# Float64 weights to float32: a bit shift of the upper word plus the scaled lower word, in place, with one work array per job

## The chip, the cores and the metric

The kernel runs on one core of a Trainium2 chip. Its time is the device time of one execution in microseconds (us); of several runs the median counts. The engines are TensorE (PE, matrix products, with its weight loads as PEld), VectorE (DVE), ScalarE (ACT), GpSimd (POOL) and SyncE (SP), which issues most of the transfers.

## The reference

The input x has 8 batches of 3008 x 256 float32. A Fourier transform runs over both axes, its real part goes through a feed-forward layer with a piecewise activation. The weights come as float64 and are used as float32 values:

```
X = np.fft.fft(x, axis=1)
X = np.fft.fft(X, axis=2)
x = X.real.astype(np.float32).reshape(24064, 256)
h = x @ w_in                       # 256 x 2048
g = np.where(h >= 1, h, np.where(h <= -1, 0.0, (h + 1) ** 2 / 4))
return (g @ w_out).astype(np.float32)   # 2048 x 256
```

## The kernel before

The transform over the sequence is split into two stages of small products (3008 = 64 x 47), the one over the 256 columns is folded into `w_in`. The feed-forward layer is cut into **units**: one batch, one of three chunks of tokens, 128 of the 2048 inner columns. There are 384 units. For each of them TensorE computes two products u and v of the first layer (`gemm1`, line 552, three passes each, in three PSUM banks by the name `uv` that are used in turn), VectorE computes `us` from the first (line 555), then the two signs `h` = us - uv and us + uv (lines 558, 559), ScalarE two passes over h (`a`), VectorE the activation step `g` out of a and h (line 574, later 579, which writes into h), and TensorE adds the second layer's product into four banks `acc` (`gemm2`, line 635) some units later. From unit 20 on, `g` is split into a rounded part `gh` (ScalarE) and a rest `gl` (GpSimd, line 598). While a batch is in the units, the transform of the next one is done in pieces in between.

Batch 0 has nothing to hide behind, so at the start the transform of batch 0, the conversion of the weights and the first units are woven together by hand. `START` is a list of steps ahead of unit 0, `AHEAD`, `AMID` and `STEPS` give the steps inside the units 0 to 32. A step is a letter and a number; up to unit 24 the order in which steps are written out is the order of issue on every engine (`pin`). The letters that matter here are: `l` load a piece of weights, `x` load a piece of x, `y` and `g` fold such a piece (VectorE and GpSimd), `p` a piece of the transform on TensorE (p0 to p7 first stage, p8 the extra row, p9 on the second stage), `w` and `z` copies of its result, `q` splits the second stage's result into `pqh` and `pql`, `F` and `f` the products that fold a converted half of `w_in` with the column transform (line 342) and round it to `wh` on ScalarE, `s` its lower part `wl` on VectorE, `u`, `O`, `Q` the rounded and the lower part of `w_out`.

The weights are 16 **jobs** of 128 x 512 float64 values each, read as pairs of 32-bit words, lower word first (`raw`). Jobs 0, 1, 4, 5, 8, 9, 12, 13 are of `w_in`, the others of `w_out`. Before, a job runs as follows. `a`: VectorE takes the 20 upper mantissa bits and the 11 exponent bits out of the upper word into the two halves of a work array `cv` (lines 253, 258). `b`: ScalarE turns the mantissa into 1.xxx and the exponent into the bits of a power of two, with clamping at both ends, in three passes (lines 267 to 269). `c`: VectorE adds the lower word times 2^-52 to the mantissa and the sign to the power (lines 274, 275). `d` on GpSimd or `v` on VectorE (jobs 0, 1, 2): mantissa times power (line 289). The work arrays lie in buffers lent by the names `h`, `a` and `gl`.

Of the kernel before, what the change touches and what calls it, by code (L numbers as in the profile page):

```python
# [22 lines left out]
P = 128  # L23
# [5 lines left out]
CH = 512  # L29
# [12 lines left out]
def _constants():  # L42
# [30 lines left out]


START = (
# [3 lines left out]
)  # L79
AHEAD = {1: "v2 G0"}  # L80
AMID = {0: "p11", 1: "p12 D1 E1 q11 q12", 3: "p13 q13", 6: "p14 q14", 7: "f2", 11: "f4", 16: "f6"}
STEPS = {
    0: "c2",
    1: "b3",
    2: "c3 d3",
    3: "a4 b4",
    4: "a5 c4 d4 b5",
    5: "c5 d5",
    7: "f3 a8 s2 b8",
    8: "s3 r1 a9 c8 d8 b9",  # L90
    9: "a6 c9 d9 b6",
    10: "c6 d6",
    11: "f5 a12 s4 b12",
    12: "s5 r2 a13 c12 d12 b13",
    13: "a7 c13 d13 b7",
    14: "c7 d7 u0",
    15: "a10 b10 L0 L1 u1 Q0",
    16: "s6 u2 Q1 |",
    17: "f7 a11 c10 d10 b11",
    18: "s7 r3 c11 d11 L2",  # L100
    19: "a14 Y0 b14 L3 u3 O2",
    20: "a15 c14 d14 b15",
    21: "O3 c15 d15 u4",
    22: "O4 Y1 u6 u5",
    23: "O6 O5 u7",
    24: "O7",
# [20 lines left out]
def fft_ffn_kernel(ctx: ExitStack, tc: tile.TileContext, x, xn, cst, w_in, w_out, out):  # L127
    nc = tc.nc

    wts = ctx.enter_context(tc.tile_pool(name="wts", bufs=1))  # L130
    sb = ctx.enter_context(tc.tile_pool(name="sb", bufs=1))
# [128 lines left out]
    def convert_fields(n):  # L260
        convert_mantissa(n)
        convert_exponent(n)

    def convert_floats(n):
        man, exp = (cv[n][0][:, i] for i in range(2))
        expf = exp.bitcast(F32)
# [10 lines left out]
    def convert_scale(n, eng):  # L277
        t, _ = cv.pop(n)
        kind, q, *_ = jobs[n]
        man, exp = (t[:, i].bitcast(F32) for i in range(2))  # L280
        dst = man
        if kind == "in":
            f32s[n] = man
        else:
            if q % 2 == 0:
                pair = sb.tile([P, 2, CH], F32, tag="gl", name=f"wo_{q // 2}", bufs=4)
                wo32[q], wo32[q + 1] = pair[:, 0], pair[:, 1]
            dst = wo32[q]
# [81 lines left out]
    s1, s2, zn = {}, {}, {}  # L370
# [302 lines left out]
    n1 = XC  # L673

    def piece_sums(n):
# [31 lines left out]
        "G": activate,
# [32 lines left out]
    for i in range(n_units + LAG):  # L740
        if i < n_units:
            b, r = divmod(i, per)
# [18 lines left out]
        first, _, then = STEPS.get(i, "").rpartition("|")  # L761
# [109 lines left out]
```

## Time and profile before

| | us |
|---|---|
| median of 3 runs | 1712.65 |
| lowest and highest run | 1712.25, 1715.63 |
| profiled execution | 1712.49 |
| its span, from the first to the last instruction | 1710.7 |
| busy in the span: PE, PEld, DVE, ACT, POOL | 1705.1, 1389.1, 1353.6, 1335.6, 1123.2 |

The 1.8 us between span and time lie around the instructions. An engine's busy time is the union of its instructions; on PE an instruction that waits in the pipeline counts as busy, so its busy time is no measure of its load. The TensorE clock was granted in full (2.4 GHz) over the whole span.

### The profile page before, as it was taken

The page shows a single profiled execution, that of the slowest core. Times are in us where ns is not written, and L with a number is a line of the kernel's source. Part 1 is how long each engine was busy: PE and PEld are TensorE (multiplying, and loading weights), DVE is VectorE, ACT ScalarE, POOL GpSimd, SP SyncE. Part 2 cuts the span into 40 slices and gives each one's busy share as a digit, 9 for nine tenths or more (in the row PEclk, how much of TensorE's full clock was granted, in tenths as well). Part 3 has the DMA queues.
Part 4 walks back from the last instruction along what each step waited for, and adds up shares of the span by engine and source line. Part 5 has one row for each costly group of instructions (what it writes and reads, how often), then busy time and mean ns, then how long its engine had stood idle before and what let it go on. Part 6 is the DMA issues. An engine that isn't in the chain of part 4 may idle for free.

```text
span 1710.7 us, 21453 instructions
## 1 busy us (share of the span) xinstructions
PE 1705.1 (100%) x7736; PEld 1389.1 (81%) x7736; DVE 1353.6 (79%) x1762; ACT 1335.6 (78%) x1541; POOL 1123.2 (66%) x921
## 2 busy tenths in 40 slices
PE   9999999999999999999999999999999999999999
PEld 6557888888888888888888888888888888888887
DVE  8998788877777787777777778777777777778776
ACT  6878777877788777887787877887778877777775
POOL 1125678856887568865688657886577855566664
PEclk9999999999999999999999999999999999999999
DMA  8123111100011000110010100101001010000000
GB/s 322 48 98 109 59 57 56 61 13 31 25 45 60 20 25 25 56 48 20 25 62 20 59 8 25 62 24 56 19 13 62 1 36 31 1 25 24 1 25 25
DMA packets 35466, 76.29 MB, mean 45 GB/s; under 512 B 4640, under 2 KB 13344, under 8 KB 35360
## 3 DMA queue, kind: packets, MB, share of 16 engines
q1 hardware_dynamic: 35180, 74.79, 12.6%
q8 instruction: 61, 1.00, 0.2%
q14 instruction: 45, 0.37, 0.1%
q10 hardware_dynamic: 180, 0.14, 0.0%
HBM read 47.10 MB, written 27.81 MB: 44 GB/s over the span
## 4 chain that ended last, share of the span: by engine, by line
PE 99%; DMA 0%; DVE 0%; SPq 0%; ACT 0%; issue 0%
PE acc L635 62%; PE uv L552 31%; PE s L509 3%; PE s L391 2%; PE s L396 1%; PE wps L342 1%; DMA raw<-in_moe_w_in_dram 0%; PE delta L321 0%; PE ny L482 0%; DVE cv L289 0%; DVE o L653 0%; DVE cv L275 0%; DVE y L153 0%; DVE cv L274 0%; DVE o L641 0%; DVE cv L253 0%
## 5 line engine op out<-in xcount | busy, mean ns | idle before, releaser
L598 POOL TENSOR_TENSOR gl<-h,gh 128x512 fp32r<-128x512 f32 (+1 forms) x724 | 908.9, 1276 | 449.2 <-PE acc L635 220.2
L564 ACT ACTIVATE a<-h,biases 128x1024 f32<-128x1024 f32 (+1 forms) x385 | 436.0, 1133 | 265.6 <-DVE h L559 264.1
L635 PE MATMUL acc<-gh,woh 128*128 128x512 f32 (+1 forms) x1456 | 574.3, 394 | 0.0
L635 PE MATMUL acc<-gl,woh 128*128 128x512 f32 (+1 forms) x1456 | 570.0, 391 | 0.0
L635 PE MATMUL acc<-gh,wol 128*128 128x512 f32 (+1 forms) x1456 | 566.9, 389 | 0.0
L555 DVE SCALAR_TENSOR_TENSOR us<-nyb,delta,uv 128x512 f32<-128x512 f32 (+1 forms) x384 | 282.9, 737 | 287.9 <-PE uv L552 287.3
L579 DVE SCALAR_TENSOR_TENSOR h<-a,h 128x1024 f32<-128x1024 f32 (+1 forms) x365 | 477.2, 1308 | 2.6 <-ACT a L565 2.1
L582 ACT ACTIVATE gh<-h 128x1024 fp32r<-128x1024 f32 (+1 forms) x365 | 379.8, 1040 | 46.6 <-DVE h L579 29.5
L565 ACT ACTIVATE a<-a 128x1024 f32<-128x1024 f32 (+1 forms) x385 | 395.1, 1026 | 1.1
L635 PEld LDWEIGHTS acc<-gl,woh 128*128 128x128 f32 x1456 | 274.3, 188 | 57.1
L635 PEld LDWEIGHTS acc<-gh,wol 128*128 128x128 f32 x1456 | 273.7, 188 | 56.4
L635 PEld LDWEIGHTS acc<-gh,woh 128*128 128x128 f32 x1456 | 273.8, 188 | 53.5
L552 PE MATMUL uv<-pqh,wh 128*128 128x512 f32 (+1 forms) x768 | 306.3, 399 | 0.0
L558 DVE TENSOR_TENSOR h<-us,uv 128x512 f32<-128x512 f32 (+1 forms) x384 | 260.3, 678 | 52.0 <-DVE us L555 1.5
L552 PE MATMUL uv<-pql,wh 128*128 128x512 f32 (+1 forms) x768 | 299.3, 390 | 0.0
L552 PE MATMUL uv<-pqh,wl 128*128 128x512 f32 (+1 forms) x768 | 298.9, 389 | 0.0
L559 DVE TENSOR_TENSOR h<-us,uv 128x512 f32<-128x512 f32 (+1 forms) x384 | 257.5, 671 | 0.0
L552 PEld LDWEIGHTS uv<-pqh,wl 128*128 128x128 f32 x768 | 144.2, 188 | 35.0 <-issue 4.6
L552 PEld LDWEIGHTS uv<-pqh,wh 128*128 128x128 f32 x768 | 144.2, 188 | 33.4 <-issue 3.6
L552 PEld LDWEIGHTS uv<-pql,wh 128*128 128x128 f32 x768 | 144.1, 188 | 30.2 <-DVE pql L220 0.4
L166 POOL TENSOR_TENSOR x<-x 120x256 f32<-120x256 f32 x72 | 68.2, 948 | 4.6 <-DVE h L579 3.5
L635 PE MATMUL acc<-g,wo 128*128 128x482 f32 (+1 forms) x160 | 69.6, 577 | 0.0
(80 smaller groups left out, 783.5 us busy)
## 6 DMA issues: line engine op xcount, KB each, us to landing
x<-in_xn_dram SPq DMA_DIRECT2D x36, 512.0 KB, 3.5
out_dram<-o SPq DMA_DIRECT2D x26, 512.0 KB, 2.8
x<-in_x_dram SPq DMA_DIRECT2D x16, 512.0 KB, 6.1
out_dram<-o SPq DMA_DIRECT2D x14, 482.0 KB, 2.9
nyb<-nyr SPq DMA_DIRECT2D x24, 256.0 KB, 3.2
raw<-in_moe_w_in_dram SPq DMA_DIRECT2D x4, 512.0 KB
raw<-in_moe_w_out_dram SPq DMA_DIRECT2D x4, 512.0 KB, 10.5
part<-o SPq DMA_DIRECT2D x4, 512.0 KB, 3.0
```

The costliest lines, as they stand in the source:

```text
L166: return nc.gpsimd.tensor_tensor(t[:, r], t[:, r], t[:, r + 1], op=ALU.add).ins
L509: nc.tensor.matmul(pt[:, i], z[:, c], rm, start=True, stop=True)
L552: nc.tensor.matmul(t[:, :n], w[m][:, cols], r[:, m, :n], start=(j == 0), stop=(j == 2))
L555: nc.vector.scalar_tensor_tensor(us, nyb[b, k][:, :n], delta[:, f : f + 1], uv[0], op0=ALU.mult, op1=ALU.add)
L558: nc.vector.tensor_tensor(h[:, 0], us, uv[1], op=ALU.subtract)
L559: last_h = nc.vector.tensor_tensor(h[:, 1], us, uv[1], op=ALU.add).ins
L564: nc.scalar.activation(a[:, sg], h[:, sg], AF.Relu, bias=half, scale=0.5)
L565: nc.scalar.activation(a[:, sg], a[:, sg], AF.Square)
L579: g = nc.vector.scalar_tensor_tensor(h[:, sg], a[:, sg], 1.0, h[:, sg], op0=ALU.min, op1=ALU.max).ins
L582: nc.scalar.activation(gh[:, sg], h[:, sg], AF.Copy)
L598: ins = nc.gpsimd.tensor_tensor(gl[:, sg], h[:, sg], gh[:, sg].bitcast(F32), op=ALU.subtract).ins
L635: nc.tensor.matmul(acc[:, :n], w, g[:, sg], start=(begin and j == 0), stop=(last and j == len(terms) - 1))
```

## The change

A float64 whose exponent lies in the range of float32 becomes a float32 when its upper word is shifted left by three bits and sign and top exponent bit are put back; what is then missing are the mantissa bits of the lower word, worth (lower word) x 2^-52 x (power of two of the value). The changed kernel computes this with one work array of 128 x 512 per job, and otherwise in place in `raw`. `e` is ScalarE's `Abs` of the upper word read as a float, `T` ScalarE's scaling of the lower word (`b` is both). `a` is now two chained steps on VectorE, a clamp of the float and shift-and-mask of its bits. `J` joins sign and bits, `K` takes sign and exponent of the joined word, that is the signed power of two (`c` is both). `M` multiplies the lower word with the power (VectorE for jobs 0 and 1, GpSimd for the others), and a sum gives the value (`v` on VectorE for jobs 0, 1, 2; `d` is scale and sum on GpSimd). The two halves of a `w_in` block and two neighbouring jobs of `w_out` share a buffer by the name `gl` (`h` for jobs 0 and 1).

```
-WORK = {1: "a", 3: "a", 4: "gl", 5: "gl", 7: "a", 8: "gl", 9: "gl", 11: "a", 12: "gl", 13: "gl", 15: "a"}
-BUFS = {"h": 4, "a": 3, "gl": 4}
+BUFS = {"h": 4, "gl": 4}
+SMALLEST, LARGEST = (float(np.uint32(n).view(np.float32)) for n in (0x38000000, 0x47EFFFFF))
...
-    def convert_mantissa(n):
-        raw = raws.pop(n)
-        tag = WORK.get(n, "h")
-        t = sb.tile([P, 2, CH], U32, tag=tag, name=f"cv_{n}", bufs=BUFS[tag])
-        high = raw[:, :, 1]
-        nc.vector.tensor_scalar(t[:, 0], high, 0xFFFFF, None, op0=ALU.bitwise_and)
-        nc.vector.tensor_scalar(t[:, 1], high, 20, 0x7FF, op0=ALU.logical_shift_right, op1=ALU.bitwise_and)
...
+    def convert_size(n):
+        raw = raws.pop(n)
+        t = work_tile(n)
+        cv[n] = t, raw
+        nc.scalar.activation(t.bitcast(F32), raw[:, :, 1].bitcast(F32), AF.Abs)
+    def convert_tail(n):
+        low = cv[n][1][:, :, 0]
+        nc.scalar.activation(low.bitcast(F32), low, AF.Copy, scale=2.0**-52)
...
     def convert_floats(n):
-        nc.scalar.activation(man.bitcast(F32), man, AF.Copy, scale=2.0**-20, bias=1.0)
-        nc.scalar.activation(expf, exp, AF.Relu, bias=above, scale=-1.0)
-        nc.scalar.activation(exp, expf, AF.Relu, bias=top, scale=-(2.0**23))
+        convert_size(n)
+        convert_tail(n)
+    def convert_fields(n):
+        nc.vector.tensor_scalar(size, size, SMALLEST, LARGEST, op0=ALU.max, op1=ALU.min)
+        nc.vector.tensor_scalar(t, t, 3, 0x3FFFFFF8, op0=ALU.logical_shift_left, op1=ALU.bitwise_and)
+    def convert_head(n):
+        nc.vector.scalar_tensor_tensor(high, high, 0xC0000000, t, op0=ALU.bitwise_and, op1=ALU.bitwise_or)
+    def convert_power(n):
+        nc.vector.tensor_scalar(t, raw[:, :, 1], 0xFF800000, None, op0=ALU.bitwise_and)
     def convert_join(n):
-        nc.vector.scalar_tensor_tensor(man, raw[:, :, 0], 2.0**-52, man, op0=ALU.mult, op1=ALU.add)
-        nc.vector.scalar_tensor_tensor(exp, raw[:, :, 1], 0x80000000, exp, op0=ALU.bitwise_and, op1=ALU.bitwise_or)
+        convert_head(n)
+        convert_power(n)
+    def convert_scale(n):
+        if n < 2:
+            nc.vector.scalar_tensor_tensor(low, raw[:, :, 0], 2.0**-52, t.bitcast(F32), op0=ALU.mult, op1=ALU.mult)
+        else:
+            nc.gpsimd.tensor_tensor(low, low, t.bitcast(F32), op=ALU.mult)
-        eng.tensor_tensor(dst, man, exp, op=ALU.mult)
+    def convert_sum(n, eng):
+        eng.tensor_tensor(t, high, low, op=ALU.add)
+    def convert_rest(n):
+        convert_scale(n)
+        convert_sum(n, nc.gpsimd)
...
-    8: "s3 r1 a9 c8 d8 b9",
+    8: "s3 r1 a8 c8 d8 b9",
```

The tables move steps of the jobs. Three places show what that does to the order of issue. The first is VectorE at the start, from the end of job 0 to the third fold of x: `x_1` and `x_2` (of 96 x 512) are the folds y1 and y2, `y_0` the fold y0. Before:

```order
L289 TENSOR_TENSOR cv_115<-cv_115 128x512
L153 TENSOR_TENSOR y_0_130<-x_0_95 96x512
L158 TENSOR_TENSOR x_0_95<-x_0_95 96x64
L274 SCALAR_TENSOR_TENSOR cv_121<-raw_92,cv_121 128x512
L275 SCALAR_TENSOR_TENSOR cv_121<-raw_92,cv_121 128x512
L153 TENSOR_TENSOR x_1_98<-x_1_98 96x512
L289 TENSOR_TENSOR cv_121<-cv_121 128x512
L153 TENSOR_TENSOR x_2_100<-x_2_100 96x512
```

The same place of VectorE's order now:

```order
L311 TENSOR_TENSOR f_in_112<-raw_87 128x512
L152 TENSOR_TENSOR y_0_121<-x_0_92 96x512
L157 TENSOR_TENSOR x_0_92<-x_0_92 96x64
L278 TENSOR_SCALAR f_in_112<-f_in_112 128x512
L279 TENSOR_SCALAR f_in_112<-f_in_112 128x512
L285 SCALAR_TENSOR_TENSOR raw_89<-raw_89,f_in_112 128x512
L290 TENSOR_SCALAR f_in_112<-raw_89 128x512
L152 TENSOR_TENSOR x_1_95<-x_1_95 96x512
L301 SCALAR_TENSOR_TENSOR raw_89<-raw_89,f_in_112 128x512
L311 TENSOR_TENSOR f_in_112<-raw_89 128x512
L152 TENSOR_TENSOR x_2_97<-x_2_97 96x512
```

Ahead of the fold of `x_1` two joins of job 1 became four chained steps, and between the folds of `x_1` and `x_2` one step became two; before, the fields of job 1 stood further up, ahead of the joins of job 0.

The second place is VectorE in unit 8, from its activation step `g` to the `us` of unit 9. Before:

```order
L574 SCALAR_TENSOR_TENSOR g_568<-a_532,h_529 128x1024
L363 SCALAR_TENSOR_TENSOR wl_71<-wps_541,biases,wh_69 128x512
L253 TENSOR_SCALAR cv_581<-raw_wol 128x512
L258 TENSOR_SCALAR cv_581<-raw_wol 128x512
L274 SCALAR_TENSOR_TENSOR cv_545<-raw_wol,cv_545 128x512
L275 SCALAR_TENSOR_TENSOR cv_545<-raw_wol,cv_545 128x512
L555 SCALAR_TENSOR_TENSOR us_598<-nyb_2_187,delta,uv_0_590 128x512
```

And now:

```order
L604 SCALAR_TENSOR_TENSOR g_556<-a_523,h_520 128x1024
L393 SCALAR_TENSOR_TENSOR wl_71<-wps_532,biases,wh_69 128x512
L278 TENSOR_SCALAR f_in_537<-f_in_537 128x512
L279 TENSOR_SCALAR f_in_537<-f_in_537 128x512
L285 SCALAR_TENSOR_TENSOR raw_wol<-raw_wol,f_in_537 128x512
L290 TENSOR_SCALAR f_in_537<-raw_wol 128x512
L585 SCALAR_TENSOR_TENSOR us_585<-nyb_2_181,delta,uv_0_577 128x512
```

The count is the same; before, the first pair was of job 9 and the second of job 8, now all four are of job 8 and each works on what the one ahead left. Jobs 4, 5, 6, 7, 9, 12, 13 stand in units 4 to 14 in the same way.

The third place is GpSimd from the last fold of x at the start to the jobs of the first units. Before, with one pass for a job:

```order
L153 TENSOR_TENSOR x_6_108<-x_6_108 96x512
L289 TENSOR_TENSOR wo_326<-cv_275 128x512
L289 TENSOR_TENSOR cv_414<-cv_414 128x512
L289 TENSOR_TENSOR cv_442<-cv_442 128x512
L289 TENSOR_TENSOR cv_545<-cv_545 128x512
```

Now there is first the scale of job 2, then two passes for each of the jobs 3, 4, 5 and so on:

```order
L152 TENSOR_TENSOR x_6_105<-x_6_105 96x512
L303 TENSOR_TENSOR raw_woh<-raw_woh,f_out_251 128x512 x2
L311 TENSOR_TENSOR f_out_251<-raw_woh 128x512
L303 TENSOR_TENSOR raw_woh<-raw_woh,f_in_406 128x512
L311 TENSOR_TENSOR f_in_406<-raw_woh 128x512
L303 TENSOR_TENSOR raw_woh<-raw_woh,f_in_406 128x512
L311 TENSOR_TENSOR f_in_406<-raw_woh 128x512
```

Over the whole kernel GpSimd's passes for the jobs go from 13 to 27, ScalarE's from 48 to 32. The transfers of SyncE stand in the same order, and behind unit 24 the order of every engine is as before.

## Rows read from the trace of the kernel before

**Rows 1.** The page: busy us, share of the span and instructions of each engine.

```profile
PE 1705.1 (100%) x7736; PEld 1389.1 (81%) x7736; DVE 1353.6 (79%) x1762; ACT 1335.6 (78%) x1541; POOL 1123.2 (66%) x921
```

**Rows 2.** The chain that ended last, in order of time: start us, us, what.

```profile
252.67 2.80 PE acc L635 x12
...
460.71 2.80 PE acc L635 x12
```

**Rows 3.** Timeline of DVE at the start: start us, length us, instruction, idle before.

```profile
5.24 0.43 DVE L253 TENSOR_SCALAR cv<-raw 128x512 uint32<-128x512 uint32 x1 [4.14 <-DMA raw<-in_moe_w_in_dram]
...
7.75 0.69 DVE L275 SCALAR_TENSOR_TENSOR cv<-raw,cv 128x512 uint32<-128x512 uint32 x1
...
8.48 0.69 DVE L289 TENSOR_TENSOR cv<-cv 128x512 f32<-128x512 f32 x1
...
9.09 0.68 DVE L153 TENSOR_TENSOR y<-x 96x512 f32<-96x512 f32 x1
...
9.80 0.22 DVE L158 TENSOR_TENSOR x<-x 96x64 f32<-96x64 f32 x1
...
11.15 0.68 DVE L153 TENSOR_TENSOR x<-x 96x512 f32<-96x512 f32 x1
...
12.35 0.68 DVE L153 TENSOR_TENSOR x<-x 96x512 f32<-96x512 f32 x1
```

**Rows 4.** Timeline of PE at the start: weight fold, third piece, product of unit 0.

```profile
13.27 1.12 PE L342 MATMUL wps<-cv,cm 128*128 128x512 f32 x2
...
14.23 0.36 PE L396 MATMUL s<-cs,x 96*128 96x96 f32 x2
...
25.13 0.48 PE L552 MATMUL uv<-pql,wh 128*128 128x482 f32 x1
```

**Rows 5.** Timeline of DVE and POOL from unit 8 to unit 9.

```profile
65.17 0.42 DVE L258 TENSOR_SCALAR cv<-raw_wol 128x512 uint32<-128x512 uint32 x1
65.50 0.69 DVE L274 SCALAR_TENSOR_TENSOR cv<-raw_wol,cv 128x512 f32<-128x512 uint32 x1
...
66.70 0.74 DVE L555 SCALAR_TENSOR_TENSOR us<-nyb,delta,uv 128x512 f32<-128x512 f32 x1
66.92 1.27 POOL L289 TENSOR_TENSOR cv<-cv 128x512 f32<-128x512 f32 x1 [12.85 <-PE uv L552]
...
68.76 1.22 DVE L574 SCALAR_TENSOR_TENSOR g<-a,h 128x1024 f32<-128x1024 f32 x1
```

**Rows 6.** Timeline of DVE and POOL, a unit of batch 0 and the last unit.

```profile
169.96 2.55 POOL L598 TENSOR_TENSOR gl<-h,gh 128x512 fp32r<-128x512 f32 x2 [2.81 <-DVE x L153]
...
171.79 1.81 DVE L579 SCALAR_TENSOR_TENSOR h<-a,h 128x1024 f32<-128x1024 f32 x1
...
1695.79 1.79 DVE L579 SCALAR_TENSOR_TENSOR h<-a,h 128x512 f32<-128x512 f32 x1 [0.20 <-ACT a L565]
...
1696.99 1.74 POOL L598 TENSOR_TENSOR gl<-h,gh 128x512 fp32r<-128x512 f32 x1
...
1697.50 1.78 DVE L579 SCALAR_TENSOR_TENSOR h<-a,h 128x512 f32<-128x512 f32 x1
```

**Rows 7.** Timeline of ACT at the start: a pass over one job, and `wh`.

```profile
7.60 0.61 ACT L267 ACTIVATE cv<-cv 128x512 f32<-128x512 uint32 x1
...
21.68 0.69 ACT L350 ACTIVATE wh<-wps,biases 128x512 fp32r<-128x512 f32 x1 [0.23 <-PE wps L342]
```

**Rows 8.** Timeline of POOL at the start: folds of x_3 and x_4.

```profile
12.61 1.55 POOL L153 TENSOR_TENSOR x<-x 96x512 f32<-96x512 f32 x1 [11.36 <-DMA x<-in_x_dram]
...
14.13 1.26 POOL L153 TENSOR_TENSOR x<-x 96x512 f32<-96x512 f32 x1
```

**Rows 9.** Timeline of DVE and PE, `us` of units 15 and 18, product of unit 16.

```profile
96.60 0.71 DVE L555 SCALAR_TENSOR_TENSOR us<-nyb,delta,uv 128x482 f32<-128x482 f32 x1
...
99.00 0.38 PE L552 MATMUL uv<-pqh,wh 128*128 128x482 f32 x1
...
111.73 0.72 DVE L555 SCALAR_TENSOR_TENSOR us<-nyb,delta,uv 128x482 f32<-128x482 f32 x1 [1.28 <-PE uv L552]
```

More of the change, by code (lines that the diff above doesn't have):

```diff
@@ L75 @@
 START = (
[3 rows of a table removed]
[3 rows of a table added]
 )
 AHEAD = {1: "v2 G0"}
-AMID = {0: "p11", 1: "p12 D1 E1 q11 q12", 3: "p13 q13", 6: "p14 q14", 7: "f2", 11: "f4", 16: "f6"}
+AMID = {0: "p11 M2", 1: "p12 D1 E1 q11 q12", 3: "p13 q13", 6: "p14 q14", 7: "f2", 11: "f4", 16: "f6"}
 STEPS = {
-    0: "c2",
-    1: "b3",
+    1: "a3",
     2: "c3 d3",
[L86 to L89, printed above, removed]
-    8: "s3 r1 a9 c8 d8 b9",
[L91 to L97, printed above, removed]
-    16: "s6 u2 Q1 |",
[L99 to L103, printed above, removed]
+    3: "b4",
+    4: "a4 c4 d4 b5",
+    5: "a5 c5 d5",
+    7: "f3 s2 b8",
+    8: "s3 r1 a8 c8 d8 b9",
+    9: "a9 c9 d9 b6",
+    10: "a6 c6 d6",
+    11: "f5 s4 b12",
+    12: "s5 r2 a12 c12 d12 b13",
+    13: "a13 c13 d13 b7",
+    14: "a7 c7 d7 u0",
+    15: "b10 L0 L1 u1 Q0",
+    16: "s6 u2 Q1 |",
+    17: "f7 a10 c10 d10 b11",
+    18: "s7 r3 a11 c11 d11 L2",
+    19: "Y0 b14 L3 u3 O2",
+    20: "a14 c14 d14 b15",
+    21: "O3 a15 c15 d15 u4",
     22: "O4 Y1 u6 u5",
@@ L200, in fft_ffn_kernel @@
     delta = wts.tile([P, NFT], F32, name="delta")
-    biases = wts.tile([P, 5], F32, name="biases")
-    for i, v in enumerate((0.5, 1151.0, 255.0 * 2**23, 1.0, 1.0)):
+    biases = wts.tile([P, 2], F32, name="biases")
+    for i, v in enumerate((0.5, 1.0)):
         nc.vector.memset(biases[:, i : i + 1], v)
-    half, above, top, one, inner = (biases[:, i : i + 1] for i in range(5))
+    half, inner = (biases[:, i : i + 1] for i in range(2))
     nc.vector.memset(inner[0:1], 0.0)
@@ L243, in load_w, with work_tile @@
         raws[n] = raw
-    cv = {}
-    def convert_mantissa(n):
+    cv, pairs = {}, {}
+    def work_tile(n):
+        kind, q, *half = jobs[n]
+        if kind == "in":
+            key, slot = ("in", q), half[0]
+        else:
+            key, slot = ("out", q // 2), q % 2
+        if key not in pairs:
+            tag = "h" if n < 2 else "gl"
+            pairs[key] = sb.tile([P, 2, CH], U32, tag=tag, name=f"f32_{kind}_{key[1]}", bufs=BUFS[tag])
+        return pairs[key][:, slot]
+    def convert_size(n):
@@ L248, in convert_mantissa @@
         raw = raws.pop(n)
-        tag = WORK.get(n, "h")
-        t = sb.tile([P, 2, CH], U32, tag=tag, name=f"cv_{n}", bufs=BUFS[tag])
-        high = raw[:, :, 1]
+        t = work_tile(n)
         cv[n] = t, raw
-        nc.vector.tensor_scalar(t[:, 0], high, 0xFFFFF, None, op0=ALU.bitwise_and)
-    def convert_exponent(n):
+        nc.scalar.activation(t.bitcast(F32), raw[:, :, 1].bitcast(F32), AF.Abs)
+    def convert_tail(n):
+        low = cv[n][1][:, :, 0]
+        nc.scalar.activation(low.bitcast(F32), low, AF.Copy, scale=2.0**-52)
@@ L256, in convert_exponent, with convert_floats @@
+    def convert_floats(n):
+        convert_size(n)
+        convert_tail(n)
+    def convert_fields(n):
+        t, _ = cv[n]
+        size = t.bitcast(F32)
+        nc.vector.tensor_scalar(size, size, SMALLEST, LARGEST, op0=ALU.max, op1=ALU.min)
+        nc.vector.tensor_scalar(t, t, 3, 0x3FFFFFF8, op0=ALU.logical_shift_left, op1=ALU.bitwise_and)
+    def convert_head(n):
         t, raw = cv[n]
         high = raw[:, :, 1]
-        nc.vector.tensor_scalar(t[:, 1], high, 20, 0x7FF, op0=ALU.logical_shift_right, op1=ALU.bitwise_and)
@@ L260, in convert_fields @@
[L260 to L266, printed above, removed]
-        nc.scalar.activation(man.bitcast(F32), man, AF.Copy, scale=2.0**-20, bias=1.0)
-        nc.scalar.activation(expf, exp, AF.Relu, bias=above, scale=-1.0)
-        nc.scalar.activation(exp, expf, AF.Relu, bias=top, scale=-(2.0**23))
+        nc.vector.scalar_tensor_tensor(high, high, 0xC0000000, t, op0=ALU.bitwise_and, op1=ALU.bitwise_or)
@@ L271, in convert_join @@
+    def convert_power(n):
+        t, raw = cv[n]
+        nc.vector.tensor_scalar(t, raw[:, :, 1], 0xFF800000, None, op0=ALU.bitwise_and)
     def convert_join(n):
+        convert_head(n)
+        convert_power(n)
+    def convert_scale(n):
         t, raw = cv[n]
-        man, exp = t[:, 0].bitcast(F32), t[:, 1]
-        nc.vector.scalar_tensor_tensor(man, raw[:, :, 0], 2.0**-52, man, op0=ALU.mult, op1=ALU.add)
-        nc.vector.scalar_tensor_tensor(exp, raw[:, :, 1], 0x80000000, exp, op0=ALU.bitwise_and, op1=ALU.bitwise_or)
@@ L277, in convert_scale @@
-    def convert_scale(n, eng):
-        t, _ = cv.pop(n)
+        low = raw[:, :, 0].bitcast(F32)
+        if n < 2:
+            nc.vector.scalar_tensor_tensor(low, raw[:, :, 0], 2.0**-52, t.bitcast(F32), op0=ALU.mult, op1=ALU.mult)
+        else:
+            nc.gpsimd.tensor_tensor(low, low, t.bitcast(F32), op=ALU.mult)
+    def convert_sum(n, eng):
+        t, raw = cv.pop(n)
         kind, q, *_ = jobs[n]
-        man, exp = (t[:, i].bitcast(F32) for i in range(2))
-        dst = man
+        low, high = (raw[:, :, m].bitcast(F32) for m in range(2))
+        t = t.bitcast(F32)
+        eng.tensor_tensor(t, high, low, op=ALU.add)
@@ L282, in convert_scale @@
         if kind == "in":
-            f32s[n] = man
+            f32s[n] = t
         else:
[L285 to L288, printed above, removed]
-        eng.tensor_tensor(dst, man, exp, op=ALU.mult)
+            wo32[q] = t
+    def convert_rest(n):
+        convert_scale(n)
+        convert_sum(n, nc.gpsimd)
     wo = {}
@@ L697, in fft_ffn_kernel @@
         "q": lambda n: stage2_split(0, n - n1 - 1),
+        "e": convert_size,
+        "T": convert_tail,
+        "b": convert_floats,
         "a": convert_fields,
-        "A": convert_mantissa,
-        "B": convert_exponent,
-        "b": convert_floats,
+        "J": convert_head,
+        "K": convert_power,
         "c": convert_join,
-        "d": lambda n: convert_scale(n, nc.gpsimd),
-        "v": lambda n: convert_scale(n, nc.vector),
+        "M": convert_scale,
+        "d": convert_rest,
+        "v": lambda n: convert_sum(n, nc.vector),
         "F": lambda n: fold_half(n, 0),
```

6 rows, old and new, of the table START are left out of this document.

## The prediction

> **What bounds the kernel now.** I read the page first. TensorE is busy over the whole span and VectorE for four fifths of it [rows 1], but a busy TensorE may also be one that waits, so the next view is the chain of work that ended last: it is TensorE nearly everywhere, and the same piece of it comes back after 208.04 us from one batch to the next [rows 2]. That is an engine which streams and waits for nobody; the order of every engine is the same from unit 24 on; so the change can act only ahead of it, and what it costs or gives TensorE there reaches the end unshortened. The third view is the timeline of that stretch. TensorE's work there is fed by VectorE's short chain at the start [rows 3, 4], and in units 4 to 15 VectorE has hardly a gap and runs behind TensorE [rows 5, 9]. The number to look for in each view is therefore not how much an engine works, but how late a result may come before TensorE stops.
>
> **Price of one step.** On VectorE a step over two arrays whose inputs are ready starts 0.60 us after the one ahead: 11.15 to 12.35 for two [rows 3]. One that needs the result of the step right ahead starts 0.73 us after it, 0.04 us behind its end (7.75 to 8.48, lasting 0.69). A step with constants lasts 0.42 us and lets the next start after 0.33 (65.17 to 65.50 [rows 5]); where the next needs its result I take 0.46, its length and the same 0.04. Before, the four steps of a job were two pairs that didn't need each other: 2 x 0.33 + 2 x 0.60 = 1.86 us. Now they are one chain in place: clamp, shift, join, power, so 0.46 + 0.46 + 0.73 + 0.33 = 1.98 us. The clamp works on floats, which no row shows: 0.42 as for integers, at most 0.69 as for a step over two arrays; I take 0.42, as it too has one array and constants.
>
> **A pair of engines that exclude each other.** Unit 9 [rows 5] shows GpSimd's 1.27 us per pass beside the sums and differences of VectorE, with the activation step g at its plain 1.22 us. In the steady state GpSimd does two passes from 0.24 us behind `us` on (169.96, 2.55 us), and g, which wants to start at 171.79, takes 1.81 [rows 6]: it begins only when GpSimd has ended. `us` and the differences, which read one operand from PSUM, aren't touched. At the end of the kernel two such steps of VectorE meet two passes of GpSimd, and they alternate: GpSimd's second, issued at 1696.99, takes 1.74 instead of 1.27, and VectorE's second, issued at 1697.50, ends at 1699.28, 0.55 us behind it.
>
> **The start.** ScalarE's `Abs` comes first: 0.61 us [rows 7] behind the landing at 5.24, so the clamp starts at 5.89. Then 0.46 + 0.46 + 0.73 + 0.46 + 0.73 + 0.60, and y0 starts at 9.33 instead of 9.09. Behind it come 0.71 us (9.09 to 9.80) and 0.15 (9.80 to 11.15 less two joins). Fields, head and power of job 1, which all stand ahead of y1 now, take another 1.98, so y1 starts at 12.17 instead of 11.15. Still ahead of y2 are job 1's scale and sum. Before, GpSimd's fold of x_3, ready at 12.61, met only the end of y2: it took 1.55 us instead of 1.26 [rows 8], so it began at 12.90, 0.55 us into y2. Now it meets y1 and takes its turn at 12.72; scale, sum and y2, all over two arrays in SBUF, then alternate with the four folds. x_3 runs to 13.98, the scale ends 0.55 later at 14.53; GpSimd starts 0.12 us ahead of such an end (1698.73 - 1.27 against 1697.58 in [rows 6]), so x_4 runs 14.41 to 15.67, the sum ends at 16.22, x_5 at 17.36, y2 at 17.91. TensorE's third piece began at 14.23 [rows 4] and can't before 17.96: 3.7 us later. Everything up to the first product follows it. A further 0.3 us comes from the `Abs` of job 2, put ahead of the rounding `wh` on ScalarE: 0.61 less the overlap of 0.09 and less the 0.23 idle there [rows 7]; VectorE's lower parts, for which TensorE waits at 25.13, are behind it. Together **4.0 us**.
>
> **Units 1 to 3.** VectorE gains a pair of constant steps ahead of `us` 2 (0.8) and a g that waits 0.15, and loses the pair a4 (0.67) and 0.13 at job 3. The two joins of job 2 (1.2) are gone as well, but the g behind them waits for ScalarE's two passes over the h of unit 0, which don't move. I count **0.1**; 1.2 less is the lower bound.
>
> **Units 4 to 15.** The work between `us` 4 and `us` 15 has no idle time. It held 7 constant pairs and 8 join pairs, 7 x 0.66 + 8 x 1.20 = 14.2 us; now 8 whole jobs, 15.8: 1.6 more. GpSimd now does two passes per job, scale and sum, 2.54 us from 0.22 behind `us` on, the geometry of 169.96: g loses 1.81 - 1.22 = 0.59 in six of these jobs and 0.1 in job 5, where a `pql` from PSUM stands in between: 3.6. `us` 15 is so late by 4.0 + 0.1 + 1.6 + 3.6 = 9.3. TensorE needs its bank again for the second product of unit 16, at 99.00; `us` 15 ended at 97.31 [rows 9], so 1.6 us are free (0.05 go into the signal), and TensorE is **7.7 us** late. Behind unit 16 VectorE had gaps of its own (at `us` 18 it waited 1.28 us for TensorE) and falls no further back.
>
> **What costs nothing.** ScalarE loses 16 of 48 passes, but its long waits were for h of VectorE; if these vanished, 0.6 us a job would count. The memsets are done long before 5.24. The work arrays no longer borrow h and a buffers, for which no view shows a wait. The matmuls are the same. Loads keep their order, and buffers come free later by one or two GpSimd passes, with units between.
>
> **What no row shows** is a GpSimd pass over every other word, as scale and sum read them. From below 1.27, as over whole rows: VectorE's steps on the same words (0.43 at 5.24, 0.69 at 65.50) cost no more than others. From above twice that, if both words were fetched: g would lose 3.2 us a job instead of 0.6, some 18 in all, 1738. I take 1.27, the nearer. The Trainium skill (GPSIMD Engine Reference, Performance pitfalls for Q7 kernels) puts a dearer price on steps above 8 bytes only; these are 8, so by it the sum stays; no run here shows it yet.
>
> **Rivals.**
> - *VectorE keeps its turn through y2* and the folds wait. The sum ends at 14.19, the weight fold of 0.96 us (13.27 to 14.23) follows, the third piece starts at 15.2: 1.0 late instead of 3.7, total 1717.5. For it: y1, scale come back to back. Against: at 1697.50 a step issued ahead of the end of its forerunner still lost its turn.
> - *GpSimd keeps its turn* through all four folds, 12.72 to 17.76; scale and sum end at 19.04, the third piece starts at 20.05, 2.1 us later than forecast: 1722.3. Against it: the alternation at 1697.
> - *Not slower: a step that needs the one ahead costs no more than another.* Then a job takes 3 x 0.33 + 0.60 = 1.59 us, 1.5 us less than before over the 8 jobs. The start goes 8.70 for y0, 11.16 for y1, 11.76, 12.36, and only y2 meets GpSimd: it ends at 14.72, the third piece is 0.5 late. 0.5 + 0.3 + 0.1 - 1.5 + 3.6 - 1.6 = 1.4: 1713.9. It decides from about a third of the 0.13 us a step. For it: that price rests on few rows. Against it: 7.75 to 8.48 in the very chain at stake. The Trainium skill (VectorE: DVE Perf Modes, The DRAIN you can't avoid) says that a semaphore between two steps costs nothing extra, which is this rival; 0.73 against 0.60 here disagrees.
> - *Dearer GpSimd passes or clamp*: 1726 and above.
> - *Faster*: needs a shorter start, and no step there gets shorter.
>
> **How the numbers follow.** The profiled execution took 1712.49 us, the median of the runs is 1712.65, so the sum needs no correction: 1712.5 + 7.7 = **1720.2 us**. Chances: forecast 0.40, VectorE keeps 0.17, GpSimd keeps 0.10, no price for chaining 0.20, dearer passes 0.10, faster 0.03. A measurement of this kernel tells about 0.2%, 3.4 us, from no change. Only the chaining rival lies within it: same 0.20, faster 0.03, slower 0.77. The range 1713.8 to 1726.0 leaves out the faster case, the lower part of that rival and most of the dearer passes, some 0.2. The likeliest case alone: 1718 to 1723.
>
> **What would show it.** At the start y2 of VectorE ending near 17.9 between stretched folds, the third piece near 18, the first product of unit 0 some 4 us late. In units 4 to 14 g at 1.8 us beside GpSimd's sum; TensorE halting behind `us` in units 12 to 16; from unit 24 on all shifted by one constant and 208.04 us a batch. Wrong if chained constant steps follow each other after 0.33, if g stays at 1.22, if the GpSimd passes aren't near 1.27, or if TensorE's lateness at unit 24 isn't the lateness at the end.

## The result, and where the 9 us went

The changed kernel took 1722.07 us (median of 4 runs, 1721.54 to 1724.43), the kernel before 1713.38 beside it (4 runs); the ratio is 1.0052, 95% interval 1.0034 to 1.0069: slower by half a percent. The forecast was 1720.2, range 1713.8 to 1726.0. The profiled execution took 1721.72 us, 9.2 more than that of before.

The page, its first line (busy us, share of the span, instructions), beside [rows 1]:

```profile
PE 1706.8 (99%) x7736; PEld 1388.5 (81%) x7736; DVE 1362.8 (79%) x1761; ACT 1323.5 (77%) x1523; POOL 1141.9 (66%) x935
```

TensorE has the same 7736 instructions and hardly more busy time in a span 9.0 us longer. So the time went into halts, and the view of waits names most of it (7.3 us; engine, its line, what it waited for: us in total, times, longest):

```profile
...
PE s L426 <- issue: 1.2, 1, 1.2
PE s L426 <- DVE y L152: 1.0, 1, 1.0
PE s L426 <- DVE x L152: 1.0, 2, 0.5
PE wps L372 <- DVE f_in L311: 0.9, 1, 0.9
PE uv L582 <- DVE us L585: 0.9, 2, 0.5
PE acc L665 <- DVE o L683: 0.9, 1, 0.9
PE uv L582 <- DVE pql L219: 0.6, 1, 0.6
PE uv L582 <- DVE h L589: 0.5, 1, 0.5
PE acc L665 <- DVE g L604: 0.3, 1, 0.3
```

The reader is to see that each of these nine happens once or twice in 1720 us. In the trace of before, the wait for `y` at the start (0.3 us) is the only one of them. A list of halts doesn't say what they cost, though, since one behind another may cost nothing. The table below does: it is how much later TensorE starts a product than it started the same product in before, both read from the timeline. A step from one column to the next is time lost for good.

| first product of unit (us in before) | 0 (24.40) | 1 (26.91) | 4 (39.72) | 13 (83.73) | 17 (104.23) | 24 (140.08) |
|---|---|---|---|---|---|---|
| changed kernel | 2.67 | 3.24 | 3.82 | 5.28 | 7.16 | 8.60 |

From unit 24 on it stays at 8.6 through the last `acc`, and the last transfers end 8.6 us later too (at 1717.9 instead of 1709.3). The other 0.4 of the span lie behind them: from there to the end of the span it is 1.8 us instead of 1.4, and no row shows what fills them. Between these steps the rows are as follows. First the start, timeline of VectorE, GpSimd and TensorE, which answers to [rows 3, 4, 8]:

```profile
9.23 0.68 DVE L152 TENSOR_TENSOR y<-x 96x512 f32<-96x512 f32 x1
...
12.07 0.68 DVE L152 TENSOR_TENSOR x<-x 96x512 f32<-96x512 f32 x1
12.67 0.68 DVE L301 SCALAR_TENSOR_TENSOR raw<-raw,f_in 128x512 f32<-128x512 uint32 x1
13.39 1.64 DVE L311 TENSOR_TENSOR f_in<-raw 128x512 f32<-128x512 f32 x1
14.95 1.75 DVE L152 TENSOR_TENSOR x<-x 96x512 f32<-96x512 f32 x1
...
12.47 2.00 POOL L152 TENSOR_TENSOR x<-x 96x512 f32<-96x512 f32 x1 [11.21 <-DMA x<-in_x_dram]
14.45 1.71 POOL L152 TENSOR_TENSOR x<-x 96x512 f32<-96x512 f32 x1
...
15.09 1.13 PE L372 MATMUL wps<-f_in,cm 128*128 128x512 f32 x2 [0.93 <-DVE f_in L311]
16.76 2.07 PE L426 MATMUL s<-cs,x 96*128 96x96 f32 x16 [0.54 <-DVE x L152]
...
28.36 0.49 PE L582 MATMUL uv<-pql,wh 128*128 128x482 f32 x1 [0.59 <-DVE pql L219]
```

y0 and y1 start 0.1 us from where the sum had put them. The sum L311 and the fold y2 are stretched, by 0.95 and 1.07 us, and end 0.56 and 0.54 us behind a GpSimd fold; the scale L301 ahead of them isn't, there it is the first GpSimd fold that takes 2.00 instead of 1.26 [rows 8]. The third piece starts at 16.76, 2.5 us late. Then one job in the full stretch, job 7 between units 14 and 15, VectorE and GpSimd, beside [rows 5]:

```profile
102.13 0.42 DVE L278 TENSOR_SCALAR f_out<-f_out 128x512 f32<-128x512 f32 x1
102.58 0.43 DVE L279 TENSOR_SCALAR f_out<-f_out 128x512 uint32<-128x512 uint32 x1
103.05 0.69 DVE L285 SCALAR_TENSOR_TENSOR raw_wol<-raw_wol,f_out 128x512 uint32<-128x512 uint32 x1
103.77 0.43 DVE L290 TENSOR_SCALAR f_out<-raw_wol 128x512 uint32<-128x512 uint32 x1
104.11 0.71 DVE L585 SCALAR_TENSOR_TENSOR us<-nyb,delta,uv 128x482 f32<-128x482 f32 x1
...
106.07 1.70 DVE L604 SCALAR_TENSOR_TENSOR g<-a,h 128x964 f32<-128x964 f32 x1
...
104.33 1.30 POOL L303 TENSOR_TENSOR raw_wol<-raw_wol,f_out 128x512 f32<-128x512 f32 x1 [3.14 <-issue]
105.71 1.04 POOL L311 TENSOR_TENSOR f_out<-raw_wol 128x512 f32<-128x512 f32 x1
```

From clamp to `us` it is 1.98 us, the steps 0.45, 0.47, 0.72 and 0.34 apart; g lasts 1.70 instead of 1.16 and ends 1.02 us behind GpSimd's sum, as a step that had to let it finish. What TensorE loses behind these steps, up to unit 17, comes in two waits; TensorE and VectorE, then the same product of TensorE in before:

```profile
104.88 0.49 PE L582 MATMUL uv<-pqh,wh 128*128 128x482 f32 x1 [0.44 <-DVE us L585]
...
107.69 1.27 DVE L683 COPY o<-acc 128x512 f32<-128x512 f32 x2
108.43 1.88 PE L665 MATMUL acc<-g,f_out 128*128 128x482 f32 x4 [0.89 <-DVE o L683]
...
101.38 3.40 PE L635 MATMUL acc<-g,wo 128*128 128x482 f32 x8
```

The second product of unit 16 waits for `us` 15 and is 5.88 us late (99.00 in [rows 9]). Then the next sum in `acc` waits until VectorE has copied the finished one out of the first bank to `o`; that copy stands behind one more stretched g, and TensorE is 7.05 us late. Last the halt ahead of unit 24, ScalarE and TensorE:

```profile
142.01 1.10 ACT L594 ACTIVATE a<-h,biases 128x964 f32<-128x964 f32 x1 [2.61 <-DVE h L589]
...
144.95 1.13 ACT L330 ACTIVATE woh<-f_out 128x512 fp32r<-128x512 f32 x2
145.99 0.36 ACT L435 ACTIVATE z<-s 64x24 f32<-64x24 f32 x2
146.36 1.33 ACT L469 ACTIVATE z<-s 64x192 f32<-64x192 f32 x4
...
147.79 1.10 PE L426 MATMUL s<-cs,x 96*128 96x96 f32 x8 [1.20 <-issue]
```

TensorE starts the next first-stage piece of batch 1 0.1 us behind the end of ScalarE's copies `z`, which empty the bank of the piece before. These stand behind `a` and two roundings, and `a` waited 2.61 us for VectorE's h. In before `z` was done 0.8 us ahead of this piece:

```profile
137.10 1.33 ACT L439 ACTIVATE z<-s 64x192 f32<-64x192 f32 x4
...
139.27 1.03 PE L396 MATMUL s<-cs,x 96*128 96x96 f32 x8
```

The profile puts the halt down to "issue": here it was the row in front, on another engine, that told more.

### The profile page after: what moved, and what is told of

The parts are those of the page before. It is cut to its first block, busy times and chain, and to the rows that moved or that the text cites. A ratio compares the mean times of both kernels' runs of the same rounds, so it can differ in the third digit from the quotient of the medians.

```text
span 1719.7 us, 21460 instructions
## 1 busy us (share of the span) xinstructions
PE 1706.8 (99%) x7736; PEld 1388.5 (81%) x7736; DVE 1362.8 (79%) x1761; ACT 1323.5 (77%) x1523; POOL 1141.9 (66%) x935
## 4 chain that ended last, share of the span: by engine, by line
PE 93%; DVE 4%; issue 1%; POOL 0%; ACT 0%; DVEq 0%; POOLq 0%
PE acc L665 59%; PE uv L582 29%; PE s L539 2%; PE s L421 2%; DVE g L604 1%; DVE us L585 1%; DVE h L589 0%; DVE h L588 0%; PE s L426 0%; PE wps L372 0%; DVE raw_wol L285 0%; DVE raw L285 0%; DVE o L683 0%; DVE f_out L279 0%; DVE wl L393 0%
## 5 line engine op out<-in xcount | busy, mean ns | idle before, releaser
L665 PE MATMUL acc<-g,f_out 128*128 128x482 f32 (+1 forms) x160 | 69.8, 579 | 1.2 <-DVE o L683 0.9
```

Source lines behind the costliest of these rows:

```text
L665: nc.tensor.matmul(acc[:, :n], w, g[:, sg], start=(begin and j == 0), stop=(last and j == len(terms) - 1))
```

## The experiments

All lateness below is read as in the table above; times are medians, with the interval of the ratio to the kernel before. Before itself had medians of 1712.39 to 1712.46 us beside them.

| first product of unit | 0 | 1 | 4 | 13 | 17 | 24 | time, us | ratio, interval |
|---|---|---|---|---|---|---|---|---|
| steps apart | 1.85 | 2.30 | 3.45 | 3.29 | 3.29 | 3.29 | 1716.56 | 1.0020 to 1.0042 |
| steps apart, scale on the last | 1.83 | 2.28 | 2.73 | 2.56 | 2.56 | 2.56 | 1715.80 | 1.0008 to 1.0029 |
| no sum on GpSimd | 2.71 | 3.28 | 3.85 | 4.36 | 4.36 | 4.70 | 1718.94 | 1.0026 to 1.0054 |
| before, two passes | 1.59 | 1.59 | 1.58 | 3.20 | 5.58 | 6.33 | 1718.65 | 1.0021 to 1.0045 |
| folds behind y2 | 1.03 | 1.62 | 2.20 | 3.64 | 5.53 | 6.96 | 1720.14 | 1.0029 to 1.0056 |
| y2 ahead | 6.32 | 6.91 | 7.48 | 8.93 | 10.81 | 12.25 | 1725.38 | 1.0059 to 1.0083 |
| Abs behind | 3.42 | 4.80 | 5.37 | 6.80 | 8.69 | 10.13 | 1723.45 | 1.0058 to 1.0083 |
| interleaved | 2.77 | 3.35 | 3.92 | 5.42 | 7.15 | 8.62 | 1721.75 | 1.0048 to 1.0074 |
| copies ahead | 9.42 | 9.42 | 10.00 | 11.45 | 13.33 | 13.74 | 1724.01 | 1.0054 to 1.0079 |
| longer warm-up | 5.42 | 6.01 | 6.57 | 8.00 | 9.90 | 11.34 | 1723.42 | 1.0046 to 1.0074 |
| steps apart and folds | 1.26 | 1.73 | 2.85 | 2.68 | 2.68 | 2.68 | 1715.00 | 1.0003 to 1.0020 |
| combined | 0.98 | 1.56 | 2.12 | 3.18 | 4.69 | 4.70 | 1718.17 | 1.0018 to 1.0038 |

**Steps apart.** Is it the waiting for the step right ahead that makes a job dear?

```diff
-  shift: t   <- t << 3 & mask      head: high <- high & top | t       power: t    <- high & mask
+  shift: high <- high << 3 & mask  head: t    <- t & top | t          power: high <- high & mask
```

> The changed kernel with the same number and kind of VectorE steps, but each reads what the step two ahead of it wrote instead of the one right ahead (shift and power work on the upper word, clamp and head on the work tile), so the weights that come out are not the converted ones. If a step that needs the one right ahead starts 0.13 us later than another (my reading), the steps follow after 0.33, 0.33, 0.60 and 0.33 us, a job takes 1.59 instead of 1.98, y0 starts 0.4 earlier and y1 0.8, us of unit 15 is some 3 us earlier, and the time falls by 4 to 5 us to about 1717. If waiting for the step right ahead costs nothing extra, gaps and time stay as they are (0.46 and 0.73; 1722).

1716.56 us. The same four steps now follow each other after 0.34, 0.33, 0.61 and 0.33 us:

```profile
98.35 0.41 DVE L278 TENSOR_SCALAR f_out<-f_out 128x512 f32<-128x512 f32 x1
98.69 0.43 DVE L279 TENSOR_SCALAR raw_wol<-raw_wol 128x512 uint32<-128x512 uint32 x1
99.02 0.69 DVE L285 SCALAR_TENSOR_TENSOR f_out<-f_out 128x512 uint32<-128x512 uint32 x1
99.63 0.43 DVE L290 TENSOR_SCALAR raw_wol<-raw_wol 128x512 uint32<-128x512 uint32 x1
99.96 0.72 DVE L585 SCALAR_TENSOR_TENSOR us<-nyb,delta,uv 128x482 f32<-128x482 f32 x1
```

A job takes 1.61 us instead of 1.98, and TensorE isn't held up once behind unit 4. Not all of the 5 us is the chain's, though: the scale needs only the head's result here, so GpSimd starts 0.12 us ahead of `us` instead of 0.22 behind it, and the g beside this job lasts 1.42 instead of 1.70. To part the two, the scale was made to read what the last step wrote:

```diff
-  scale (GpSimd): low <- low * t
+  scale (GpSimd): low <- low * high
```

> As the run in which each conversion step reads what the step two ahead of it wrote (the weights are again not the converted ones), but GpSimd's scale now reads what the last of the four steps wrote, as in the changed kernel; in the earlier run it read the third's and so began 0.36 us sooner, which shortened g from 1.70 to 1.40 as well. Here only the chaining is gone. If the price of chaining is 0.13 us a step by itself, g is back at 1.65 to 1.70, a job still takes 1.59 instead of 1.98, TensorE is 3.3 us late from unit 4 on as there, 4 to 5 late at unit 17, and the time 1717.5 to 1719. If most of the 5 us gained there came from GpSimd's earlier start, 1720 or more.

1715.80, but the parting failed: with both operands in one array GpSimd's scale took 1.04 us instead of 1.30, and g stayed at 1.41 to 1.46. What stands is the arithmetic of VectorE's rows up to `us` 15: 0.37 us less a job is 3.0 us over 8 jobs, about 0.27 less a g is 1.6 over six. How TensorE's 5 us divide between the two isn't shown.

**No sum, and two passes before.** Does GpSimd's second pass stretch g? Once taken away, once added to the kernel before:

```diff
-  convert_scale(n); convert_sum(n, nc.gpsimd)
+  convert_scale(n)
```

> The changed kernel without the sums on GpSimd: from job 3 on only the scale is left there, so the weights lack the upper part of the sum. If g is stretched because the second GpSimd pass holds the pair of engines (my reading), every g lasts 1.16 or 1.22 us, us of unit 15 is 3.4 us earlier, TensorE does not halt in units 12 to 17 and at unit 23, and its lateness stays at the 3.8 us that it has from unit 4 on: about 1716.5. If g is stretched by something else (the scale, or the sums of its own job), it stays at 1.67 to 1.72 and the time near 1722.

```diff
+  eng.tensor_tensor(exp, man, exp, op=ALU.mult)
   eng.tensor_tensor(dst, man, exp, op=ALU.mult)
```

> The kernel before with one more GpSimd pass per job ahead of its product (exponent times mantissa into the exponent's array, so the weights come out wrong), nothing else altered. If the second pass alone costs what I think, g lasts about 1.8 instead of 1.2 us in seven jobs of units 4 to 14, 4 us in all; less 1.6 us that were free at unit 16 TensorE is 2.5 late there, and the jobs of units 17 to 21 add up to 1.5: 1715 to 1716.5. If GpSimd's passes are hidden, 1712.5.

Without the sum (1718.94 us, the profiled execution 1717.67) every g of units 4 to 21 lasts 1.16 or 1.22 us, and the halts in units 16, 17 and 24 are gone but for 0.3; the gain is less than expected, since the chain alone still costs 0.5 around unit 12 and 0.3 at unit 24. With two passes in before, timeline of unit 9:

```profile
68.94 0.74 DVE L557 SCALAR_TENSOR_TENSOR us<-nyb,delta,uv 128x512 f32<-128x512 f32 x1
...
70.98 1.89 DVE L576 SCALAR_TENSOR_TENSOR g<-a,h 128x1024 f32<-128x1024 f32 x1
...
69.15 1.28 POOL L290 TENSOR_TENSOR cv<-cv 128x512 f32<-128x512 f32 x1 [11.38 <-PE uv L554]
70.51 1.28 POOL L291 TENSOR_TENSOR cv<-cv 128x512 f32<-128x512 f32 x1
```

g is stretched by 0.67 (in the changed kernel by 0.44 to 0.56), and the steps come at the same units as there, 1.6 by unit 13, 2.4 by unit 17, 0.75 at unit 24. The time is above the expectation: the kernel lost 4.7 us from unit 4 on against 4 expected, and 1.6 more at the start of this profiled execution, to TensorE's clock (below). So a second pass alone, longer than the changed kernel's sum but without any chain, brings a loss behind unit 4 as large as the change does (4.8).

**Folds behind y2.** Is the start lost by taking turns?

```diff
-  p1 y2 w0 w1 p8 f0 p2 g3 w2
+  p1 y2 H3 w0 w1 p8 f0 p2 w2        (H: the same fold on GpSimd, waiting for VectorE's last step so far)
```

> The changed kernel with one wait added: GpSimd's four folds of x_3 to x_6 wait for the end of y2 on VectorE, so that scale, sum and y2 have the pair of engines for themselves. If the start is lost by taking turns, y2 ends at 14.7 instead of 16.70, the weight fold f0 runs from 14.1 to 15.1, the third piece starts at 15.1 instead of 16.76, the folds end at 19.8 instead of 19.05, which is still ahead of the pieces that need them, and the first product of unit 0 starts at 25.4 instead of 27.07: 1720.0. If the folds themselves pace the start, the first product comes 0.7 us later than in the changed kernel: 1722.4.

1720.14 us, timelines of VectorE, GpSimd and TensorE:

```profile
12.66 0.68 DVE L301 SCALAR_TENSOR_TENSOR raw<-raw,f_in 128x512 f32<-128x512 uint32 x1
13.37 0.69 DVE L311 TENSOR_TENSOR f_in<-raw 128x512 f32<-128x512 f32 x1
13.98 0.68 DVE L152 TENSOR_TENSOR x<-x 96x512 f32<-96x512 f32 x1
...
14.74 4.94 POOL L152 TENSOR_TENSOR x<-x 96x512 f32<-96x512 f32 x4 [13.49 <-DVE x L152]
...
15.08 2.11 PE L426 MATMUL s<-cs,x 96*128 96x96 f32 x16
```

Nothing is stretched, the third piece starts at 15.08, the first product 1.64 us earlier, and these 1.6 us are kept to the end. An added wait made the kernel faster.

**y2 ahead.** The other way out, to put the fold that TensorE waits for ahead of job 1's scale and sum:

```diff
-  y1 M1 v1 p1 y2 w0 w1 p8 f0 p2 g3 w2 s0 ... p3 F1 g4 w3 p4 g5 w4 p5
+  y1 p1 y2 w0 w1 p8 p2 g3 M1 v1 w2 ... p3 g4 w3 f0 p4 F1 g5 w4 s0 p5
```

> The changed kernel with only the order of the start altered: the fold y2 stands right behind y1 on VectorE and the third piece of the first stage ahead of the weight fold f0; scale and sum of job 1 come behind them, beside the GpSimd folds. If the 2.5 us lost at the start come from taking turns with GpSimd (my reading), y2 starts near 12.7 and ends near 13.4, the third piece starts near 14 instead of 16.76, the first product of unit 0 near 25.3 instead of 27.07, and the time falls by 1.5 to 2 us to about 1720. If instead the longer chain of the conversion itself is what arrives late, the first product stays near 27 and the time near 1722.

Slower, 1725.38. The third piece did start early, at 14.49. But y2 met the fold of x_3 (1.75 us), scale and sum met x_5 and x_6, the weight fold f0 came at 19.06 behind a halt of 2.50 us, and then TensorE ran at half speed (stretch of the trace, PE, PEld, DVE, ACT, POOL busy, PEclk the granted clock, DMA):

```profile
16.00:18.00 2.00, 0.56 (x5) 0.39 (x4) 1.97 (x2) 0.96 (x3) 2.00 (x2) 0.85 1.03 389
18.00:20.00 2.00, 0.94 (x1) 0.50 (x2) 1.96 (x4) 0.00 (x0) 0.45 (x1) 0.50 0.64 237
20.00:22.00 2.00, 2.00 (x8) 1.41 (x7) 0.40 (x2) 0.60 (x1) 0.00 (x0) 0.50 0.39 121
```

So the reading of the start is not refuted by it, but neither was it shown by it: the turns went to other steps. The folds behind y2 show it.

**Abs behind, copies ahead, interleaved.** Three orders that should each have taken one term away:

```diff
-  w7 e2 f1 a2 s1
+  w7 f1 e2 a2 s1

-  22: "O4 Y1 u6 u5"
+  22: "O4 Y1"          23, behind the differences: "u6 u5"

-  VectorE: us, h, h, g, clamp, shift, head, power
+  VectorE: us, clamp, h, h, shift, g, head, power
```

> The changed kernel with ScalarE's Abs of job 2 behind the rounding wh instead of ahead of it. If TensorE's wait of 0.59 us for the lower parts at 28.36 comes from this pass, it is gone or at most 0.1, units 1 to 3 come 0.5 us earlier, and the time falls by up to 0.5 us, less if VectorE, whose steps of job 2 then start 0.7 us later, is what unit 3 waits for. If not, nothing moves: 1721.6.

> The changed kernel with the two roundings u5 and u6 of the second weights (1.13 us on ScalarE) moved from ahead of the copies of batch 1's first-stage bank to behind them. If TensorE's halt of 1.2 us at 147.8 is a wait for that bank, which ScalarE empties late because VectorE brings it its h late, the first stage of batch 1 starts at 146.7, TensorE's lateness at unit 24 is 7.4 to 7.6 us instead of 8.6, and the time 1720.5. If the halt has another cause (GpSimd's fold for batch 1), it stays and so does the time, 1721.6.

> The changed kernel with the clamp of each job from job 4 on moved between us and the differences of VectorE, and the shift between the differences and g; ScalarE's two passes of some jobs stand one unit earlier so that they are there. The steps and the result are those of the changed kernel. Two of a job's three waits for the step right ahead are gone: 0.26 us, and 0.1 more where us was waited for, per job. If the price of chaining is right, us of unit 15 is 2 to 3 us earlier and the time 1718.5 to 1719.5. If order does not matter, 1721.6; if the differences now come so late that TensorE waits for their banks, above 1722.

*Abs behind* was worse: TensorE's halt for `pql` grew from 0.59 to 1.4 us (3.42 to 4.80 in the table). VectorE's order has job 2's clamp and shift, then `wl`, then `pql`, and the clamp waits for this `Abs`, so a later `Abs` is a later `pql`. So the pass doesn't cost time through `wh`: it does so through job 2, which stands on VectorE ahead of `pql`. (The other 0.75 of its start is TensorE's clock, 0.50 from 12 to 18 us.) *Copies ahead* did what it should where it acts: 13.33 to 13.74 at unit 24, 13.95 a unit later, 0.6 instead of 1.44. Its total can't show it, since in all of its executions the mean granted clock was below 1 (0.994 to 0.998); in the one profiled it was 0.50 from 12 to 31 us. *Interleaved* gained nothing:

```profile
71.09 0.74 DVE L596 SCALAR_TENSOR_TENSOR us<-nyb,delta,uv 128x512 f32<-128x512 f32 x1
71.75 1.14 DVE L285 TENSOR_SCALAR f_in<-f_in 128x512 f32<-128x512 f32 x1
...
71.31 1.30 POOL L314 TENSOR_TENSOR raw_wol<-raw_wol,f_in 128x512 f32<-128x512 f32 x1 [11.67 <-ACT f_out L266]
```

The clamp, 0.42 us elsewhere, takes 1.14 beside GpSimd's scale of the job before: it too has to let a pass finish. Six of the stretched g became plain in return, and three clamps waited 1.8 us in all for ScalarE. By the Trainium skill (SBUF — State Buffer, Who interferes with whom) a step with one array and constants can need the port pair that GpSimd uses; the 1.14 here agree.

**Longer warm-up, steps apart and folds, combined.**

```diff
-  keep_warm(5, warm)
+  keep_warm(7, warm)
```

> The changed kernel with seven instead of five products that keep TensorE busy ahead of the first piece, nothing else. In runs so far the granted clock between 11 and 18 us or later was 0.5 where TensorE had stood still for 1.6 us or more ahead of the first piece, and 1.0 where it was 1.3 us or less. If that pause brings the clock down, every execution stays at 1.0 here and takes 1721.5 to 1721.8. If the fall has another cause, some executions are again at 1722.4 to 1724.4.

> The changed kernel with both edits that took the most away: the conversion steps read what the step two ahead wrote (so the weights are not the converted ones), and the folds of x_3 to x_6 wait for y2. If the start and the later units are separate costs, they add: 1716.5 less 1.6 is 1714.9, TensorE 1.7 us late from unit 4 on and never later. If the units had only been late because of the start, the second edit gives less than 1 us here.

> The changed kernel, result unchanged, with all orders that helped: folds behind y2, the two roundings behind the copies of batch 1, seven warm products; and each job's clamp ahead of g instead of behind it, which takes one of the three waits for the step right ahead out of a job (0.13 us each, and g starts when GpSimd's sum is nearer its end). 1.6 from the start, 0.8 at unit 24 and up to 1 in units 4 to 16: 1718.2 to 1719.3. It stays above the kernel before, since two chained waits a job and GpSimd's sum remain. If the later units give back what the start gains, 1721.

The longer warm-up alone moved the fall of the clock but didn't prevent it: no pause was left ahead of the first piece, and the clock fell between 14 and 16 us, behind the pause of 0.92 for f0 (0.50 from 16 to 22 us); 1723.42, executions from 1721.62 to 1728.09. The expectation that the first pause alone does it is wrong. Steps apart and folds added up as separate costs should, 1715.00 for 1714.9. The combination took 1718.17 (1718.05 to 1718.28 in 7 executions), at full clock throughout the start of the profiled one. With the two roundings behind the copies its TensorE loses 0.2 us at units 24 and 25 instead of 1.44. It is the fastest form of the changed kernel with the same result, and still 0.28% slower than before.

## Why the prediction was right, and where not

The result is 1.9 us above the forecast, 1.5 in the profiled execution. The mechanism is the one given, a longer chain of VectorE and a g stretched by GpSimd, but the waits that the sum names make only 5.9 of the 9.2 us, and that the total came near is in part luck.

- *Price of a step*: right. 0.45 to 0.47 behind a step with constants and 0.72 to 0.73 behind one over two arrays, clamp included, as taken. The rival that chaining costs nothing is out: taking the chain away brought 5 us together with what it does to g. The Trainium skill (VectorE: DVE Perf Modes, The DRAIN you can't avoid) says, of copies, that a semaphore between two steps costs nothing extra; 0.46 against 0.33 and 0.72 against 0.61 in these two traces disagree.
- *The start, 4.0*: mechanism right, size 3.2 (unit 1 in the table). The step that failed is that scale, sum and y2 each lose a turn. The scale, asked for at 12.67 when the fold had waited since 12.47, kept the pair, and only sum and y2 lost theirs: y2 ended at 16.70 instead of 17.91. So it lay between the forecast and the rival that VectorE keeps its turn. The 0.3 for `Abs` was 0.57, and not through `wh`: the clamp of job 2 waits for this pass, and `pql` stands behind the clamp.
- *Units 1 to 3, 0.1*: 0.6. The wait of g for ScalarE at unit 1 was 0.79 instead of the 0.15 assumed, and at unit 4 TensorE waited for the second g.
- *Units 4 to 16, 3.6*: 3.3 (3.82 to 7.16), but not by the forecast wait alone. Chaining took 1.98 a job as computed; g is stretched by 0.44 to 0.56 instead of 0.59, as the sum is a pass of 1.04 us, not 1.27. With the smaller start `us` 15 is so 7.5 late (104.11 against 96.60) instead of 9.3, and TensorE behind it 5.9 at unit 16 instead of 7.7. The other 1.3 up to the 7.16 of unit 17 come from VectorE's copies `o` out of `acc`, a wait that the prediction left out. That 7.16 lies near 7.7 is luck.
- *GpSimd's price, which no row showed*: 1.30 and 1.04, at the lower end. The Trainium skill (GPSIMD Engine Reference, Performance pitfalls for Q7 kernels) puts a dearer price on steps above 8 bytes only; 1.30 and 1.04 at a step of 8 bytes, against 1.27 over whole rows, agree.
- *"Behind unit 16 VectorE had gaps and falls no further back"*: this step failed, and it cost 1.44 us at unit 24. The gap in [rows 9] was at unit 18; behind it come three more jobs and three more stretched g, `us` 22 is 9.25 us late where TensorE is 7.16, and ScalarE, which waits for its h, empties TensorE's bank too late. Without the sum, or without the chain, the step is 0.3 or nothing.

So TensorE is 1.8 us less late at unit 16 than the sum had it. The copies `o` (1.3), the halt at unit 24 (1.4), the 0.4 behind the last transfers and 0.2 outside the span are in no term of it; with the 1.8 taken off they make the 1.5 above the forecast, whose end is better than its terms.

## What to carry to other kernels

Work that is hidden by another engine has a threshold, not a price: here some 0.6 us more per job (0.12 of chain, 0.5 of a stretched g) cost nothing from unit 4 to unit 11 and then 3.3 us up to unit 17. So follow the lateness of the slower engine from where it grows to every later place where the fast one needs it, through third engines too, and not only to the first. And where two engines exclude each other, look at the order of their turns before looking at the work: making GpSimd wait was worth 1.6 us.

## What the runs showed of the hardware

- GpSimd's pass over every other word of one array took 1.04 us when both operands lay in that array (sum; scale in one experiment), and 1.30 when one lay in another; whole rows took 1.27 [rows 5].
- Who gets the pair next stays open. With a fold of GpSimd waiting since 12.5, a scale asked for at 12.67 kept it, and the fold y2, asked for at 12.68 in another run, lost it (1.75 us). The form of the two steps differs; which form decides wasn't tried.
- TensorE's granted clock fell to 0.50 (1.2 of 2.4 GHz) for 3 to 20 us near the start of some executions, each time in or behind a pause: of 1.5 to 2.0 us ahead of the first piece (no sum, two passes, Abs behind, copies ahead, steps apart and folds), of 0.9 ahead of f0 (longer warm-up), of 2.5 (y2 ahead). The profiled execution of the changed kernel kept 1.00 with pauses of 1.0 and 0.9, so a pause alone doesn't tell. The level shows in the times: with the longer warm-up, executions with a mean clock of 1.000 took 1721.6 to 1721.9 us, one with 0.995 took 1728.1. So a median here can lie up to 3 us from the profiled execution that the lateness is read from (copies ahead, 1724.01 against 1727.15).
